# Attention over 32-token segments: one memory row per segment in place of eight, TensorE's order fixed by hand, and a reordered start

## Chip, cores, metric

One core of one Trainium2 chip. The metric is the device time of one execution in microseconds (us), the median of several runs.

## The reference, cut to what matters

```python
# x: (1, 2048, 1024); 32 heads of 128; segments of 32 tokens; 8 memory rows
xn = layernorm(x)
mem = mem0
for s in range(64):                      # one segment after the other
    h = concat([mem, xn[segment s]])     # 8 + 32 rows
    q, k, v = h @ Wq, h @ Wk, h @ Wv
    p = softmax(mask(q @ k.T) * scale)   # memory rows see all columns but later ones are masked
    o = (p @ v) @ Wo
    mem = o[:8];  out[segment s] = o[8:]
g = silu((sigmoid(xn @ w_gate) * (xn @ w_up)) @ w_down)
return x + out * g
```

The kernel does not walk the 64 segments in turn. It estimates each segment's memory from sums of V (in every segment but the first the eight memory rows come out equal), does all segments in parallel, checks at the end that the estimate was good, and has a sequential fallback for the case that it was not. The fallback is not taken with these inputs. The work is therefore almost all matmul: V, q and k projections, the attention itself, gate/up and down of the gated unit (GLU), and the output projection.

## The kernel before

Start: x goes out on the sync queue, Wv at the same time on the gpsimd queue; layernorm, transposition to xnT, then V.

```python
for t in range(NT):
    nc.sync.dma_start(xall[:, t, :], x2[t * P:(t + 1) * P, :])
...
for cg in range(8):
    nc.gpsimd.dma_start(wv_sb[:, :, cg * 512:(cg + 1) * 512], Wv2[...])
...
nc.sync.dma_start(xnT_dram, xnT[:])                 # 4 MB, read by the fallback alone
...                                                 # V, 4 token tiles at a time, two staging buffers
nc.sync.dma_start(vx_dram[t0 * P:(t0 + TG) * P, ...], v_sb[:])
```

Attention: three segments are packed into a tile of 3 x (32 tokens + 8 memory rows) = 120 rows; 22 tiles per head, in batches of at most 4. The text goes head by head, and a scheduler in the build decides the order of each engine's instructions.

```python
for h in heads:
    ...                                             # q and k projections of this head (psb tiles, ACT copies)
    for b0 in range(0, NT3, NB):                    # NB = 4
        for j in range(nb): nc.tensor.matmul(s_ps[:, j, :], lhsT=qt[...], rhs=kt[...])     # scores
        # softmax: DVE add mask, max, subtract; ACT exp; DVE sum, reciprocal, multiply -> pr_
        for j in range(nb): nc.tensor.transpose(pt_ps[:, j, :], pr_[:, j, :], ident[...])  # transposes
        nc.scalar.copy(pt[...], pt_ps[...])
        for j in range(nb): nc.tensor.matmul(o_ps[:, j, :], lhsT=va[...], rhs=pt[:, j, :]) # outputs
        ...                                         # ACT copy to otx, DVE copy of one memory row to omq
    ...                                             # now and then a unit of 64 GLU gate/up matmuls
```

After the last head come the remaining GLU units, the memory check (output projection of the memory rows, 256 matmuls), and the down and output projections.

## Time and profile before

| | before |
|---|---|
| median time | 1795.9 us (12 runs, 1794.1 to 1802.0) |
| span of the profiled run | 1793.8 us |
| TensorE busy | 96% |

The page's first part, of the kernel before: busy time, share of the span, number of instructions.

```profile
span 1793.8 us, 28090 instructions
...
PE 1724.6 (96%) x11673; PEld 884.1 (49%) x11673; DVE 831.8 (46%) x1989; ACT 569.6 (32%) x1243; POOL 22.1 (1%) x60
```

The 96% say little. A matmul's recorded duration is longer than the distance to the next one: the page gives 381 ns for one of 512 columns, while the next starts 216 ns later. Any wait of TensorE shorter than the difference does not show as idle time. The Trainium skill warns of exactly this ("Trainium Kernel Development and Optimization", § Performance Expectations: matmul busy time is a bad measure, because matmuls are pipelined), and this trace agrees. So I use another measure throughout: the distance from the start of one matmul to the start of the next. For each source line and column count I take the median distance and call the sum over all matmuls the *work*; what a stretch lasts beyond its work is its *waiting*.

The windows view of the kernel before, cut at the first and last matmul of each stage (start to the last V matmul; memory estimate; attention and the GLU after it; memory check to the end). Columns: stretch, length, busy time of each engine with instruction counts, granted clock, DMA share, GB/s.

```profile
0.00:277.90 277.90, 255.12 (x1659) 112.94 (x1660) 76.76 (x153) 57.15 (x96) 8.32 (x17) 0.99 0.40 142
277.90:427.10 149.20, 138.06 (x1295) 74.80 (x1294) 28.99 (x42) 23.40 (x39) 5.91 (x33) 0.99 0.59 183
427.10:1355.60 928.50, 903.44 (x6530) 497.44 (x6529) 654.35 (x1684) 469.95 (x1076) 7.39 (x8) 1.00 0.33 95
1355.60:1793.80 438.20, 427.99 (x2194) 198.91 (x2192) 71.70 (x110) 19.11 (x32) 0.49 (x2) 0.99 0.39 103
```

By the measure above these four stages hold 240.0, 133.9, 863.1 and 426.4 us of work. The waiting is 26.0 us in the first stage once the first matmul (at 12.2 us) has started, 14.9, 65.4 and 5.3 us.

### The profile page before, as it was taken

The page shows a single profiled execution, that of the slowest core. Times are in us where ns is not written, and L with a number is a line of the kernel's source. Part 1 is how long each engine was busy: PE and PEld are TensorE (multiplying, and loading weights), DVE is VectorE, ACT ScalarE, POOL GpSimd, SP SyncE. Part 2 cuts the span into 40 slices and gives each one's busy share as a digit, 9 for nine tenths or more (in the row PEclk, how much of TensorE's full clock was granted, in tenths as well). Part 3 has the DMA queues.
Part 4 walks back from the last instruction along what each step waited for, and adds up shares of the span by engine and source line. Part 5 has one row for each costly group of instructions (what it writes and reads, how often), then busy time and mean ns, then how long its engine had stood idle before and what let it go on. Part 6 is the DMA issues. An engine that isn't in the chain of part 4 may idle for free.

```text
span 1793.8 us, 28090 instructions
## 1 busy us (share of the span) xinstructions
PE 1724.6 (96%) x11673; PEld 884.1 (49%) x11673; DVE 831.8 (46%) x1989; ACT 569.6 (32%) x1243; POOL 22.1 (1%) x60
## 2 busy tenths in 40 slices
PE   5999998999999999999999999999999999999998
PEld 3344444544555555555555555555445444444443
DVE  7121211212967788767966778876512111111111
ACT  4111111112655455555655455555310000000000
POOL 1000000010000000000000000000100000000000
PEclk9999999999999999999999999999999999999999
DMA  9722216357223323313334332230464434443440
GB/s 335 251 71 71 71 71 223 107 191 163 77 83 89 89 76 98 104 40 85 77 89 133 80 77 70 68 88 36 184 262 112 124 98 103 108 124 89 98 122 25
DMA packets 220044, 200.06 MB, mean 112 GB/s; under 512 B 70528, under 2 KB 193408, under 8 KB 217736
## 3 DMA queue, kind: packets, MB, share of 16 engines
q1 hardware_dynamic: 213768, 174.10, 33.9%
q0 software_dynamic: 6144, 24.12, 3.6%
q8 instruction: 93, 1.52, 0.4%
q14 instruction: 39, 0.32, 0.1%
HBM read 133.19 MB, written 65.01 MB: 110 GB/s over the span
## 4 chain that ended last, share of the span: by engine, by line
PE 86%; DMA 6%; ACT 4%; DVE 3%; issue 1%; SPq 0%; ACTq 0%; DVEq 0%
PE pr L457 24%; PE a_ps L591 12%; PE v_ps L339 11%; PE y_ps L583 11%; PE u_ps L90 10%; PE g_ps L86 8%; PE o_ps L504 3%; PE pt_ps L499 2%; DMA wo_t<-in_A_Wo_dram 2%; ACT pt L501 2%; PE s_ps L480 2%; DMA xall<-in_A_x_dram 2%; PE sv_ps L346 1%; DMA vx_dram<-v_sb 1%; DVE ssum L491 1%
## 5 line engine op out<-in xcount | busy, mean ns | idle before, releaser
L457 PE MATMUL pr<-xnT,wq 128*128 128x480 bf16 (+1 forms) x1280 | 247.4, 336 | 0.0
L339 PE MATMUL v_ps<-wv_sb,xnT 128*128 128x512 bf16 x1024 | 242.2, 381 | 4.7 <-ACT v_sb L344 4.7
L457 PE MATMUL pr<-xnT,wk 128*128 128x480 bf16 (+1 forms) x1280 | 243.1, 336 | 0.0
L86 PE MATMUL g_ps<-xnT,wg 128*128 128x512 bf16 x896 | 228.3, 380 | 1.4 <-DVE vm_sb L393 1.2
L591 PE MATMUL a_ps<-wo_sb,ot 128*128 128x512 bf16 x1024 | 226.2, 379 | 0.0
L90 PE MATMUL u_ps<-xnT,wu 128*128 128x512 bf16 x896 | 222.2, 379 | 1.4 <-DVE hst L94 0.7
L583 PE MATMUL y_ps<-wd,ht 128*128 128x512 bf16 x896 | 200.5, 381 | 1.0 <-DMA ht<-hT_dram 1.0
L591 PEld LDWEIGHTS <-ot 128*128 128x128 bf16 x1024 | 100.2, 98 | 120.8
L457 PEld LDWEIGHTS <-wk 128*128 128x128 bf16 x1280 | 110.8, 98 | 86.2
L457 PEld LDWEIGHTS <-wq 128*128 128x128 bf16 x1280 | 111.3, 98 | 84.8
L586 ACT ACTIVATE th<-y_ps 128x512 f32<-128x512 f32 x32 | 19.1, 597 | 407.3 <-PE y_ps L583 407.3
L94 DVE SCALAR_TENSOR_TENSOR hst<-th,u_ps 128x512 bf16<-128x512 f32 x112 | 76.1, 681 | 155.9 <-PE u_ps L90 153.8
L583 PEld LDWEIGHTS <-ht 128*128 128x128 bf16 x896 | 87.8, 98 | 107.6 <-issue 1.6
L339 PEld LDWEIGHTS <-xnT 128*128 128x128 bf16 x1024 | 90.7, 97 | 93.3 <-issue 3.2
L501 ACT COPY pt<-pt_ps 120x480 bf16<-120x480 bf16 x192 | 101.2, 527 | 100.9 <-PE pt_ps L499 98.6
L90 PEld LDWEIGHTS <-wu 128*128 128x128 bf16 x896 | 84.2, 98 | 85.3 <-issue 1.9
L93 ACT ACTIVATE th<-g_ps 128x512 f32<-128x512 f32 x112 | 67.2, 600 | 182.2 <-PE g_ps L86 182.1
L342 DVE CAST v_sb<-v_ps 128x512 bf16<-128x512 f32 x64 | 44.0, 690 | 173.9 <-PE v_ps L339 163.4
L86 PEld LDWEIGHTS <-wg 128*128 128x128 bf16 x896 | 83.7, 98 | 80.9 <-issue 3.3
L460 ACT CAST qt<-pr 128x480 bf16<-128x480 f32 (+1 forms) x160 | 78.1, 498 | 128.9 <-PE pr L457 128.9
L489 ACT ACTIVATE e<-sm 120x480 f32<-120x480 f32 x192 | 107.7, 571 | 35.1 <-DVE sm L486 34.3
L482 DVE TENSOR_TENSOR sm<-s_ps,maskb 120x480 f32<-120x480 f32 x192 | 112.2, 609 | 10.4 <-PE s_ps L480 10.4
(679 smaller groups left out, 1580.2 us busy)
## 6 DMA issues: line engine op xcount, KB each, us to landing
wo_t<-in_A_Wo_dram SPq DMA_DIRECT2D x16, 1024.0 KB
vx_dram<-v_sb SPq DMA_DIRECT2D x32, 512.0 KB
oT_dram<-otx SPq DMA_DIRECT2D x16, 1024.0 KB
ot<-oT_dram SPq DMA_DIRECT2D x16, 1024.0 KB
va<-vx_dram SPq DMA_DIRECT2D x16, 1008.0 KB
hT_dram<-hst SPq DMA_DIRECT2D x28, 512.0 KB
ht<-hT_dram SPq DMA_DIRECT2D x16, 896.0 KB
wv_sb<-in_A_Wv_dram POOLq DMA_DIRECT2D x8, 1024.0 KB, 21.5
```

The costliest lines, as they stand in the source:

```text
L86: nc.tensor.matmul(g_ps[:], lhsT=wg[:, c, fc * P:(fc + 1) * P], rhs=xnT[:, c, tb * TB:(tb + 1) * TB], start=(c == 0), stop=(c == KC - 1))
L90: nc.tensor.matmul(u_ps[:], lhsT=wu[:, c, fc * P:(fc + 1) * P], rhs=xnT[:, c, tb * TB:(tb + 1) * TB], start=(c == 0), stop=(c == KC - 1))
L93: nc.scalar.activation(th[:], g_ps[:], ACTF.Tanh, scale=0.5)
L94: nc.vector.scalar_tensor_tensor(hst[:, :, fc, :], th[:].rearrange("p (a b) -> p a b", b=P), 1.0, u_ps[:].rearrange("p (a b) -> p a b", b= ...
L339: nc.tensor.matmul(v_ps[:], lhsT=xnT[:, c, t * P:(t + 1) * P], rhs=wv_sb[:, c, cg * 512:(cg + 1) * 512], start=(c == 0), stop=(c == KC - 1))
L457: nc.tensor.matmul(pr[:, 0:ntok], lhsT=w_[:, c, hh * DH:(hh + 1) * DH], rhs=xnT[:, c, tok0:tok0 + ntok], start=(c == 0), stop=(c == KC - 1))
L460: nc.scalar.copy(dst[:, bT:bT + bn, 0:TX], pr[:, 0:bn * TX].rearrange("p (T j) -> p T j", j=TX))
L482: nc.vector.tensor_tensor(sm[:, 0:nb, :], s_ps[:, 0:nb, :], maskb[:].unsqueeze(1).to_broadcast([TR, nb, TR]), op=ALU.add)
L489: nc.scalar.activation(e[:, 0:nb, :], sm[:, 0:nb, :], ACTF.Exp, scale=scale)
L501: nc.scalar.copy(pt[:, 0:nb, :], pt_ps[:, 0:nb, :])
L583: nc.tensor.matmul(y_ps[:], lhsT=ht[:, c, :], rhs=wd[:, c, hf * 512:(hf + 1) * 512], start=(c == 0), stop=(c == FC - 1))
L591: nc.tensor.matmul(a_ps[:], lhsT=ot[:, h, :], rhs=wo_sb[:, h, hf * 512:(hf + 1) * 512], start=(h == 0), stop=(h == H - 1))
```

## The change

A segment's eight equal memory columns act in the softmax like one column of eight times the weight, so one column with log 8 added to its scaled score can stand for them. `DEPTHS` holds, in us, D1 (from scores to transposes), D2 (from transposes to outputs) and GAP (before a head's first scores).

The intent: fewer rows in the attention matmuls, a TensorE order in which every softmax and copy has room, and a start in which x is not held up by Wv. GLU, V, down and output matmuls are the same.

```diff
-TM = SPT * M
-TR = TX + TM                       # 120 rows
+TR = TX + SPT                      # 99 rows
+LN8B = 2.0794415416798357 * (128.0 ** 0.5)
-NB = 4
+NB = 5
+DEPTHS = (4.5, 1.8, 0.6)
 # --- mask: a memory column stands for eight equal ones, so it gets + log 8
+    nc.gpsimd.memset(maskb[:, TX:TR], LN8B)
 # --- start
             nc.sync.dma_start(xall[:, t, :], x2[t * P:(t + 1) * P, :])
+            if extra_dma is not None and t == min(3, NT - 1):
+                extra_dma(0)       # first slice of Wv, same queue; the other seven after x
-        nc.sync.dma_start(xnT_dram, xnT[:])
+        nc.gpsimd.dma_start(xnT_dram, xnT[:])
-                    if t % 2 == 0:
+                    if t % 2 == 0 and cg > 0:
                         nc.vector.tensor_copy(v_sb[:, tl, :], v_ps[:])
-                nc.sync.dma_start(vx_dram[...], v_sb[:])
+                nc.gpsimd.dma_start(vx_dram[...], v_sb[:])
 # --- memory rows stored once, not eight times
-            nc.sync.dma_start(vm3[1:NSEG, ...], vm_sb[1:NSEG, 0, :].unsqueeze(1).to_broadcast([NSEG - 1, M, 512]))
+            nc.sync.dma_start(vm_dram[:, cg * 512:(cg + 1) * 512], vm_sb[0:NC, 0, :])
 # --- attention: projections and GLU become generators that yield after every matmul
+        def att_s(h, b): ...       # scores and softmax of batch b
+        def att_t(h, b): ...       # transposes and their copy
+        def att_o(h, b): ...       # outputs
+        with tc.manual_schedule(engines={mybir.EngineType.PE}):
+            ...
+            for h in range(H - 1):
+                for b in range(nbat):                        # 5 batches, spread over the head's period
+                    t0_ = now + GAP + b * (period - GAP) / nbat
+                    due += [(t0_, 0, h, b), (t0_ + D1, 1, h, b)]   # transposes D1 = 4.5 us later
+                for dt in region(h):                         # projections of head h + 1 and GLU chunks
+                    now += dt
+                    run_due()                                # outputs are due D2 = 1.8 us after transposes
 # --- segment 0, whose eight memory rows differ, is done apart for all heads at the end
+        for h0 in range(0, H, 8): ...
```

The clock `now` counts projection and GLU matmuls only.

## The prediction

> **What bounds it now.** The page shows TensorE busy 96% of 1793.8 us, but those ends are modelled, so I measured from one matmul's start to the next in the trace. Medians: 216 ns for 512 columns, 202 for 480, 56 for 128, 52 to 55 for 120, 32 for 72, 25 for 4. Time is streamed columns, as the Trainium skill says ("TensorE: Matmul & The Clock Gate": back to back, N columns cost about N cycles); the trace agrees. The medians sum to 1667 us. The rest: 12.2 us before the first matmul, about 7 after the last, 108 us of start-to-start time above the medians ("excess"): 17 before t = 70, 12 to 260, 15 from 260 to 400, 66 in attention (400 to 1290), 5 around the memory check (1350 to 1390). In attention it recurs per head pair: 0.9 us at a probability transpose, 0.8 at a gate matmul, 0.2 before many output matmuls, because each softmax follows its scores too closely in TensorE's in-order program.
>
> **What changes, costed.**
> 1. Eight equal memory rows per segment become one with a log 8 bias: tiles go from 120 to 99 rows, 22 to 21 per head; segment 0 is done apart (96 matmuls of 40 columns). 2112 score, transpose and output matmuls at 54 ns = 114 us become 2016 at an estimated 45 (between 32 for 72 columns and 54 for 120) plus 2.4 us. With the 96-column projection pieces TensorE's static sum falls 19 us, all critical.
> 2. TensorE's order in attention is fixed by hand: transposes 4.5 us after scores, outputs 1.8 us later, projection and GLU between. The softmax chain (four VectorE passes near 0.6 us, a 0.57 us Exp) takes under 4 us; VectorE falls to an estimated 64%. I expect 15 us of excess left of 66: gain 51, the largest term.
> 3. Start. Now x (sync queue) and Wv (gpsimd queue) share the DMA; the last x tile lands at 36.6 us at 360 GB/s. Afterwards x and the first Wv slice go first: x lands near 17 us, the first transpose is at 8.5 us instead of 12.2. LayerNorm (1.8 us a tile) and TensorE's 2.3 us a tile bound it then. Gain 15; but V stores now share the gpsimd queue, the third behind the 4 MB xnT store, which may stall V with its two buffers some 7 us near t = 55. Net 8.
> 4. Memory-row stores shrink from 4 MB to 0.6: gain 1. The rest is unchanged.
>
> Sum: 19 + 51 + 8 + 1 = 79 us.
>
> **Prediction: 1718 us, 8 in 10 between 1700 and 1740.** Faster by over 2%: 0.96; within 2%: 0.03; slower: 0.01.
>
> **What would show it.** Step 1: 2016 matmuls of 99 columns, 44 to 47 ns start to start. Step 2: waits of transposes on VectorE under 10 us; 23.9 us of matmul work per head, about 24.4 measured. Step 3: last x tile by 18 us; first V matmul by 12 us; V evictions waiting on a V store near 50 to 65 us. Step 4: no wait for weights at the memory check, as 52 us of GLU still cover them.
>
> **What would make it wrong.** Hand delays too short, so that every batch waits (32 heads x 5 batches x 0.3 us = 48 us); 99-column matmuls not scaling with columns; the V-store stall above 7 us; ScalarE's queue delaying the copies that free the four shared PSUM buffers.

## More of the kernel before

What waiting in attention looks like: the timeline of TensorE in the kernel before (start us, busy us, group of like instructions).

```profile
703.94 0.38 PE L86 MATMUL g_ps<-xnT,wg 128*128 128x512 bf16 x1
704.16 0.40 PE L499 MATMUL pt_ps<-ident,pr__7716 120*120 120x120 bf16 x4
704.39 0.81 PE L86 MATMUL g_ps<-xnT,wg 128*128 128x512 bf16 x3
705.20 0.37 PE L504 MATMUL o_ps<-pt,va 120*128 120x120 bf16 x4
705.41 0.38 PE L499 MATMUL pt_ps<-ident,pr__7749 120*120 120x120 bf16 x4
```

Between the four transposes at 704.16 and their outputs at 705.20 there are only three GLU matmuls. They need 3 x 216 = 648 ns, but from 704.39 to 705.20 it is 810 ns: TensorE stood for 160 ns until ScalarE had copied the transposes. The busy column covers it (0.81 us). That happens in most batches: matched batch by batch in the trace, the outputs begin within 0.1 us of the end of the copy in 162 of 192; the copy ends 0.87 us (median) after the start of the last transpose and the outputs begin 0.92 us after it. The waits view, which counts only visible idle time, has 11.2 us of it:

```profile
PE pt L65 <- DVE xn L62: 14.6, 3, 12.2
PE o_ps L504 <- ACT pt L501: 11.2, 18, 0.7
```

And the softmax itself is slow. VectorE's timeline in the kernel before:

```profile
760.05 0.17 DVE L493 RECIPROCAL rs<-ssum 120x4 f32<-120x4 f32 x1
760.14 0.62 DVE L485 TENSOR_REDUCE mx<-sm 120x4 f32<-120x480 f32 x1
760.68 0.65 DVE L495 TENSOR_TENSOR pr__8507<-e,rs 120x480 bf16<-120x480 f32 x1
...
761.48 0.65 DVE L486 TENSOR_TENSOR sm<-sm,mx 120x480 f32<-120x480 f32 x1
762.04 0.97 DVE L482 TENSOR_TENSOR sm<-s_ps,maskb 120x480 f32<-120x480 f32 x2
```

One pass takes about 0.65 us, but a reciprocal and a multiply of one batch (L493, L495) alternate here with the maximum and subtract of a second (L485, L486) and the mask of a third (L482): batches arrive in a bunch, and each is served between the others. From a batch's last score matmul to its finished probabilities it takes 9.4 us (median; 6.2 to 13.2).

## The result, and the profile after

| | before | after |
|---|---|---|
| median time | 1795.93 us (12 runs) | 1699.99 us (8 runs, 1696.2 to 1703.3) |
| ratio | | 0.9465, 95% interval 0.9454 to 0.9477 |
| span of the profiled run | 1793.8 us | 1698.1 us |

A ratio is the mean time of one kernel's fast runs over that of the other's of the same rounds, so not quite the ratio of the medians that are quoted.

The windows view of the changed kernel, cut at the same four stages:

```profile
0.00:264.30 264.30, 252.78 (x1660) 111.26 (x1660) 71.29 (x146) 61.66 (x104) 25.14 (x41) 1.00 0.42 150
264.30:411.40 147.10, 137.50 (x1294) 75.34 (x1293) 29.06 (x42) 23.64 (x39) 4.01 (x21) 0.99 0.58 175
411.40:1262.10 850.70, 850.18 (x6531) 474.04 (x6530) 591.43 (x1424) 434.84 (x896) 7.43 (x8) 1.00 0.33 96
1262.10:1698.10 436.00, 426.87 (x2194) 198.39 (x2192) 71.83 (x110) 19.11 (x32) 0.49 (x2) 0.99 0.36 104
```

By the starts of the matmuls at the cuts (the windows are rounded to 0.1 us) the first stage gained 13.7 us, the second 1.9, attention 77.9 and the last 2.1. In attention the work fell from 863.1 to 846.2 us (16.9) and the waiting from 65.4 to 4.4 us (61.0).

The waits view has nothing left of outputs on ScalarE, and 0.5 us of transposes on VectorE:

```profile
PE pt L70 <- DVE xn L67: 8.4, 1, 8.4
PE wos_ps L290 <- DMA wo_t<-in_A_Wo_dram: 7.4, 8, 1.3
PE sv_ps L386 <- DVE v_sb L382: 2.8, 1, 2.8
...
PE pt_ps L526 <- DVE pr__14533 L158: 0.5, 1, 0.5
```

TensorE's timeline in the changed kernel, one batch's outputs and the next batch's pieces:

```profile
706.21 0.35 PE L541 MATMUL o_ps<-pt,va 99*128 99x99 bf16 x4
706.40 0.57 PE L494 MATMUL pr<-xnT,wk 128*128 128x480 bf16 x2
706.81 1.89 PE L95 MATMUL g_ps<-xnT,wg 128*128 128x512 bf16 x8
708.53 0.35 PE L518 MATMUL s_ps<-kt,qt 128*99 128x99 bf16 x4
708.72 0.36 PE L494 MATMUL pr<-xnT,wk 128*128 128x480 bf16 x1
708.92 0.35 PE L526 MATMUL pt_ps<-ident,pr__8011 99*99 99x99 bf16 x4
709.11 1.92 PE L494 MATMUL pr<-xnT,wk 128*128 128x480 bf16 x15
710.87 0.23 PE L505 MATMUL pm<-cmT,wk 128*128 128x72 bf16 x2
710.93 0.35 PE L541 MATMUL o_ps<-pt,va 99*128 99x99 bf16 x4
```

The transposes of 708.92 have their outputs at 710.93, and ScalarE's copy between them ended at 709.86 (709.37 + 0.49): 1 us to spare. Every start follows its predecessor at the predecessor's own rate. VectorE now works on one batch at a time (the changed kernel; these are the scores of 708.53):

```profile
708.92 0.57 DVE L145 TENSOR_TENSOR sm<-s_ps,maskb 99x396 f32<-99x396 f32 x1 [0.90 <-PE s_ps L518]
709.53 0.57 DVE L147 TENSOR_REDUCE mx<-sm 99x4 f32<-99x396 f32 x1
710.13 0.57 DVE L148 TENSOR_TENSOR sm<-sm,mx 99x396 f32<-99x396 f32 x1
711.36 0.56 DVE L153 TENSOR_REDUCE ssum<-e 99x4 f32<-99x396 f32 x1 [0.66 <-ACT e L151]
...
712.17 0.57 DVE L158 TENSOR_TENSOR pr__8069<-e,rs 99x396 bf16<-99x396 f32 x1
```

Matched batch by batch over all batches (192 before, 160 after):

| median us | before | after |
|---|---|---|
| last score matmul to finished probabilities | 9.4 | 4.2 |
| last score matmul to first transpose | 10.2 | 5.0 |
| last transpose to end of its copy | 0.87 | 0.79 |
| last transpose to first output | 0.92 | 1.97 |

So the softmax, although it lasts less than half as long, also has its transposes waiting half as long after the scores. What grew is the room after the transposes, and the room that is left over: 0.9 us after the probabilities, 1.1 us after the copy.

### The profile page after: what moved, and what is told of

Its sections match the earlier page's. It is cut to its first block, busy times and chain, and to the rows that moved or that the text cites. A ratio compares the mean times of both kernels' runs of the same rounds, so it can differ in the third digit from the quotient of the medians.

```text
span 1698.1 us, 27515 instructions
## 1 busy us (share of the span) xinstructions
PE 1667.3 (98%) x11673; PEld 859.0 (51%) x11673; DVE 763.6 (45%) x1722; ACT 539.3 (32%) x1071; POOL 37.1 (2%) x72
## 4 chain that ended last, share of the span: by engine, by line
PE 95%; DMA 3%; DVE 1%; issue 0%; ACT 0%; DVEq 0%
PE pr L494 26%; PE a_ps L683 13%; PE v_ps L379 12%; PE y_ps L675 11%; PE u_ps L104 11%; PE g_ps L95 11%; DMA wo_t<-in_A_Wo_dram 2%; PE pt_ps L526 2%; PE s_ps L518 2%; PE o_ps L541 2%; PE sv_ps L386 1%; PE pm L505 1%; PE vmr_ps L428 1%; DMA vx_dram<-v_sb 1%; PE wos_ps L290 1%; PE wo_ps L274 0%
## 5 line engine op out<-in xcount | busy, mean ns | idle before, releaser
L494 PE MATMUL pr<-xnT,wk 128*128 128x480 bf16 (+2 forms) x1280 | 257.4, 336 | 0.0
L494 PE MATMUL pr<-xnT,wq 128*128 128x480 bf16 (+2 forms) x1280 | 257.0, 336 | 0.0
L95 PE MATMUL g_ps<-xnT,wg 128*128 128x512 bf16 x896 | 220.4, 379 | 0.0
L145 DVE TENSOR_TENSOR sm<-s_ps,maskb 99x396 f32<-99x396 f32 (+2 forms) x164 | 96.3, 587 | 66.7 <-PE s_ps L518 45.2
L153 DVE TENSOR_REDUCE ssum<-e 99x4 f32<-99x396 f32 (+2 forms) x164 | 95.6, 583 | 67.1 <-ACT e L151 66.5
L528 ACT COPY pt<-pt_ps 99x396 bf16<-99x396 bf16 (+1 forms) x160 | 81.0, 506 | 103.2 <-PE pt_ps L526 101.3
L151 ACT ACTIVATE e<-sm 99x396 f32<-99x396 f32 (+2 forms) x164 | 89.9, 548 | 67.2 <-DVE sm L148 65.1
L382 DVE CAST v_sb<-v_ps 128x512 bf16<-128x512 f32 x56 | 38.7, 692 | 158.4 <-PE v_ps L379 153.3
```

The source lines that it names most:

```text
L95: nc.tensor.matmul(g_ps[:], lhsT=wg[:, c, fc * P:(fc + 1) * P], rhs=xnT[:, c, tb * TB:(tb + 1) * TB], start=(c == 0), stop=(c == KC - 1))
L145: nc.vector.tensor_tensor(smv, s_ps, maskb.unsqueeze(1).to_broadcast([R, nb, W]), op=ALU.add)
L151: nc.scalar.activation(ev, smv, ACTF.Exp, scale=scale)
L153: nc.vector.tensor_reduce(ssum[0:R, 0:nb], ev, axis=AX.X, op=ALU.add)
L494: nc.tensor.matmul(pr[:, 0:ntok], lhsT=w_[:, c, hh * DH:(hh + 1) * DH], rhs=xnT[:, c, tok0:tok0 + ntok], start=(c == 0), stop=(c == KC - 1))
L528: nc.scalar.copy(pt[:, 0:nb, :], pt_ps[:, 0:nb, 0:TR])
```

## The experiments

All 15 runs were correct. The kernel before ran beside each group, at 1795.0 to 1795.6 us. The theory: in attention the spread order of TensorE removes the waiting, and the removed rows give their columns. The main rival: fewer elements and fewer batches relieved VectorE, and the order matters little.

### text_order: the changed kernel with attention written head by head

```diff
-        with tc.manual_schedule(engines={mybir.EngineType.PE}):
-            ...                       # the interleaving
+        for h in range(H):
+            for _ in proj(h): pass
+            for b in range(nbat):
+                att_s(h, b); att_t(h, b); att_o(h, b)
+            while glu_done < ((h + 1) * n_glu_h) // H: ...   # GLU chunks
```

> The changed kernel with its attention written head by head as before (projection, then every batch's scores, transposes and outputs, then GLU), no pinned order; tiles stay 99 rows, so the matmul work is that of the changed kernel. Theory A (the spread order made the gain in attention): the scores bunch again, the outputs come some 0.9 us after their transposes, and 40 to 60 us of waiting return: 1740 to 1760 us. Rival B (fewer and smaller softmax passes relieved VectorE, and the order matters little): under 1712 us.

Measured: 1749.7 us, 49.7 us above the changed kernel. The attention stage took 898.4 us with the same work (846.3 us), so 52.1 us of waiting are back:

```profile
413.00:1311.40 898.40, 893.60 (x6530) 463.73 (x6529) 533.72 (x1424) 424.09 (x896) 7.43 (x8) 1.00 0.31 92
```

The scores bunch again (the built order has the 21 score matmuls of a head's five batches within some 40 matmuls), the softmax lasts 8.4 us (median), and the outputs follow the last transpose after 0.87 us, as soon as the copy allows. The theory holds. 52.1 is less than the 65.4 us of before, but how much of the 13.3 us the rows took with them stays open: the built order is not that of before either (there the 22 score matmuls of a head lie within 76 matmuls), and the GLU comes in chunks of 8 matmuls in place of units of 64.

### sched_order: the interleaved text without the pin

```diff
-        with tc.manual_schedule(engines={mybir.EngineType.PE}):
+        with ExitStack():
```

> The changed kernel with its interleaved text but without the pin: the scheduler may reorder TensorE. Its order as built keeps scores about 5 us ahead of transposes and transposes about 1.8 us ahead of outputs. Theory A1 (how the text is interleaved is what counts): within 8 us of the changed kernel, 1700 to 1708 us. Theory A2 (the pin itself is needed): 1730 us or more.

Measured: 1701.4 us, attention stage 850.3 us. It is the interleaving of the text that counts; the scheduler, given that text, keeps nearly the same order.

### d1_short, d2_short, d1_long: the two distances

```diff
-DEPTHS = (4.5, 1.8, 0.6)
+DEPTHS = (3.5, 1.8, 0.6)      # d1_short
+DEPTHS = (4.5, 0.4, 0.6)      # d2_short
+DEPTHS = (6.0, 1.8, 0.6)      # d1_long
```

> The changed kernel with the distance from scores to transposes cut from 4.5 to 3.5 us. In the changed kernel's trace the softmax takes 4.19 us (median) from the last score matmul and has 4.97 us of room; with 1 us less room in each of 160 batches the missing time adds to 55 us. Theory A (TensorE waits exactly for what the chain lacks): 1740 to 1760 us, as waits of transposes on VectorE. Rival B: under 1712 us.

> The changed kernel with the distance from transposes to outputs cut from 1.8 to 0.4 us. The eviction of the transposes ends 0.79 us (median) after the last transpose and has 1.97 us of room; 1.4 us less leaves 0.3 us lacking in each of 160 batches, 47 us in sum. Theory A: 1735 to 1755 us, as waits of outputs on ScalarE. Rival B: under 1712 us.

> The changed kernel with the distance from scores to transposes raised from 4.5 to 6.0 us. Only 4.4 us of start-to-start time above the medians is left in attention. Theory A (no waiting is left to remove at 4.5): within 4 us of the changed kernel, 1696 to 1704 us. Rival: softmaxes of neighbouring batches now overlap on VectorE and lengthen each other, and waits return, 1715 us or more.

Measured: d1_short 1795.8 us, d2_short 1754.1 us, d1_long 1702.9 us.

With d1_short one microsecond less gives back the whole gain of the change: the attention stage took 945.5 us, 94.9 more. The direction and place are as expected (in all 160 batches the transposes start within 0.1 us of the finished probabilities), the size (55) is not. The reason is in the order: the clock counts projection and GLU matmuls only, and the microsecond that fell out of the window also held attention matmuls of other batches. In matmul work the room shrank from 4.96 to 3.74 us (medians), by 1.22, not 1.0. The softmax took 4.24 us, so about 4.24 + 0.06 - 3.74 = 0.56 us lack in each of 160 batches, 90 us.

With d2_short the attention stage took 904.7 us, 54.1 more (expected 47), and in all 160 batches the outputs start within 0.1 us of the end of the copy. The waits view of d2_short names it; the sum there is smaller because it sees only idle time:

```profile
PE o_ps L541 <- ACT pt L528: 30.1, 129, 0.3
```

With d1_long nothing is won: 849.8 us in attention. At 4.5 us hardly any wait was left.

### rows120, rows120_long, nb4: the rows

rows120 undoes the removal of rows inside the hand order (eight rows, no log 8, batches of 4, hence 6 per head); rows120_long gives it D1 = 6.0; nb4 keeps 99 rows and has 6 batches.

```diff
-TR = TX + SPT
+TM = SPT * M
+TR = TX + TM
-NB = 5
+NB = 4                        # nb4: this line alone
-DEPTHS = (4.5, 1.8, 0.6)
+DEPTHS = (6.0, 1.8, 0.6)      # rows120_long alone
 ...                           # mask, memory loads and copies as before, eight times
```

> The changed kernel with the eight equal memory rows per segment put back (tiles of 120 rows, no log 8 bias, memory rows stored and loaded eight times, batches of at most 4 tiles, so 6 per head), the order by hand kept. Theory A (the static step is columns, and the hand order has room for a longer chain): 2016 matmuls at 54 in place of 47 ns add 14 us, waits add 0 to 12: 1713 to 1727 us. Rival B (fewer softmax elements on VectorE are worth as much as the order): waits add 30 us or more, 1740 us and above.

> The 120-row tiles in the hand order (1744.4 us, 44 slower than the changed kernel where 14 were expected) with the distance from scores to transposes raised from 4.5 to 6.0 us. In its trace the softmax takes 4.70 us (median), up to 6.8, with 5.2 us of room. Theory C (the missing 30 us are softmaxes that outlast their room): waits mostly go, 1714 to 1726 us. Theory D (VectorE, busy 85% in that stage, cannot keep up with TensorE however far ahead the scores are): 1736 us or more.

> The changed kernel (99 rows) with at most 4 tiles in a batch, so 6 batches per head in place of 5, as the 120-row kernel has. Theory C/D (the rows' elements lengthen the softmax or load VectorE; the number of batches matters little): 1699 to 1707 us. Theory E (six batches, closer together, are what made the 120-row kernel wait): 1715 us or more.

Measured: rows120 1744.4 us, rows120_long 1724.1 us, nb4 1703.2 us. The first was a miss for the theory: 44 us, of which only 14 are columns. The windows view over the attention stage, rows120 first, then rows120_long:

```profile
413.60:1300.50 886.90, 867.33 (x6425) 491.89 (x6529) 704.77 (x1648) 462.48 (x992) 7.41 (x8) 1.00 0.36 97
```

```profile
414.60:1280.10 865.50, 865.35 (x6529) 494.46 (x6528) 704.97 (x1648) 452.39 (x992) 7.41 (x8) 1.00 0.36 99
```

VectorE's busy time is the same 705 us in both, so VectorE does keep up. With 120 rows the softmax takes 4.7 us (median), up to 6.8, and 5.2 us of room is not enough: 886.9 us less the work (860.4, from the trace of rows120_long, which has all its records) leaves 26.5 us of waiting. With 6.9 us of room 5.1 us are left. Six batches instead of five cost nothing by themselves (nb4: 849.5 us in attention). So the rows' second effect is on the length of the softmax, and a longer distance buys it off.

This gives a square of four attention stages (us), and below it a third row with the longer distance:

| | 120 rows | 99 rows |
|---|---|---|
| head by head | 928.5 (before) | 898.4 (text_order) |
| order by hand, D1 = 4.5 | 886.9 (rows120) | 850.6 (changed) |
| order by hand, D1 = 6.0 | 865.5 (rows120_long) | 849.8 (d1_long) |

At D1 = 4.5 the order is worth 41.6 us with 120 rows and 47.8 with 99; the rows are worth 30.1 us head by head and 36.3 in the order by hand. The third row changes the reading: with D1 = 6.0 the order is worth 63.0 us with 120 rows, and the rows only 15.7, little more than their 14.2 us of columns. What the rows gained beyond their columns in the order by hand was room for the softmax, and a longer distance gives the same. The upper row compares two head-by-head texts that were built into different orders (see text_order). The 99-row cells also have segment 0 apart and other batch sizes, and rows120 has 21 tiles plus segment 0 rather than 22, so the columns differ in a little more than rows.

### start_only and wv_pool: the start

start_only is the kernel before with the start's part of the diff. wv_pool is the changed kernel with Wv back on the gpsimd queue at once:

```diff
-            if extra_dma is not None and t == min(3, NT - 1):
+            if extra_dma is not None and t == 0:                                 # all eight slices issued here
 ...
-                nc.sync.dma_start(wv_sb[:, :, cg * 512:(cg + 1) * 512], ...)
+                nc.gpsimd.dma_start(wv_sb[:, :, cg * 512:(cg + 1) * 512], ...)   # all eight, beside x
```

> The kernel before with the new start alone (x and the first Wv slice first on one queue, V stores and the xnT store on the gpsimd queue, first V evictions all on ScalarE). In the two traces the last V matmul starts 13.6 us earlier afterwards. Theory A (the start's gain stands by itself and is handed on to the end): 10 to 16 us faster than before, 1779 to 1786 us. Rival (it is given back later, where the old attention order waits anyway): under 6 us, 1789 us or more.

> The changed kernel with Wv loaded as before, on the gpsimd queue beside x on the sync queue; all else of the new start kept. Theory A (the shared DMA delays x and is most of the start's gain): the last x tile lands near 36 us again, the last V matmul starts 8 to 14 us later, 1708 to 1715 us. Rival (moving the V stores and the first evictions is most of it): under 1704 us.

Measured: start_only 1785.0 us, 10.0 below the kernel before beside it; its last V matmul starts 12.5 us earlier, its last matmul 9.0 us earlier (the second stage and attention are 1.7 and 1.5 us longer than before). wv_pool 1714.4 us, 14.4 above the changed kernel and 12.6 above its second measurement (after_again); its last V matmul starts at 278.0 us (before: 277.9, after: 264.2). Moving this one load back undoes the whole gain of the start. Of the 13.8 us, 3.8 are lost before the first matmul (12.2 in place of 8.4 us) and 6.9 more up to the last transposes of xn, where the work waits for x; 2.4 more are lost after that, before t = 70, where a V store is again late (16.0 us to land). The lines of the x tile's view, in before, after and wv_pool; VectorE's first pass over x, with first and last start at the end:

```profile
L54 DVE BATCH_NORM_STATS2 st<-xall x32: 639/674/694, 3.8 to 40.2; 128x6 f32<-128x512 bf16 x32
...
  DMA xall<-in_A_x_dram: 10.8, 10
```

```profile
L59 DVE BATCH_NORM_STATS2 st<-xall x32: 636/672/695, 3.5 to 31.5; 128x6 f32<-128x512 bf16 x32
...
  DMA xall<-in_A_x_dram: 2.7, 2
```

```profile
L58 DVE BATCH_NORM_STATS2 st<-xall x32: 637/676/696, 3.5 to 39.5; 128x6 f32<-128x512 bf16 x32
...
  DMA xall<-in_A_x_dram: 9.9, 10
```

Two queues with work share the bandwidth. The Trainium skill says so ("DMA: Bandwidth & Descriptors", § Queues, rings and completion order: each DMA engine goes round between the queues that have work), and the runs agree: with Wv on a second queue VectorE waits for x ten times, with Wv behind x on the same queue twice.

### xnt_late, best, after_again, vbuf3, vbuf3_wo3: the V store that lands late

In the changed kernel V's matmuls lose 2.8 us at t = 53, while ScalarE and VectorE wait for a staging buffer whose V store took 12.8 us to land (median 3.4). xnt_late moves the text of the xnT store behind the V stage; best puts it on the sync queue and gives the streamed Wo three buffers; vbuf3 leaves the DMA alone and gives V three staging buffers; vbuf3_wo3 adds the third Wo buffer.

```diff
-        nc.gpsimd.dma_start(xnT_dram, xnT[:])
+        nc.sync.dma_start(xnT_dram, xnT[:])                                    # best
-        wos = es.enter_context(tc.tile_pool(name="vg_wo", bufs=2))
+        wos = es.enter_context(tc.tile_pool(name="vg_wo", bufs=3))             # best, vbuf3_wo3
-                v_sb = sb.tile([P, TG, 512], BF16, name="v_sb", tag="v_sb")
+                v_sb = sb.tile([P, TG, 512], BF16, name="v_sb", tag="v_sb", bufs=3)  # vbuf3, vbuf3_wo3
```

> The changed kernel with the 4 MB xnT store (needed by the fallback path alone) issued after the V stage, so that no V store queues behind it. In the changed kernel V's matmuls lose 2.8 us at t = 53 while the third V store takes 12.8 us to land instead of 3.4. Theory A (the xnT store ahead in the queue is the cause): that wait goes, 2 to 4 us faster than the changed kernel, 1694 to 1698 us. Rival (the loads of the other queue are the cause): the wait stays.

> The changed kernel with the xnT store on the sync queue, so that V stores no longer queue behind it on the gpsimd queue (the earlier edit for this did not move the store: the scheduler put it back third), and three buffers in place of two for the streamed Wo. Theory A (its place ahead in the same queue made the 2.8 us wait): no wait of V evictions on a V store; Wo waits of 7.4 us fall to 4 to 6: 1692 to 1697 us. Rival (the DMA's total load made it): the wait stays, 1697 us or more.

> The changed kernel itself, as the base on the same chip for the two runs beside it: 1697 to 1702 us, with the 2.8 us wait of V's matmuls near t = 53.

> The changed kernel with three V staging buffers in place of two; every DMA is issued as before. Theory F (the third V store is late because all loads and stores of that stretch share the DMA, and what turns lateness into a wait is having only two buffers): no wait of V evictions on a V store, 2 to 4 us faster than the changed kernel beside it. Rival (the wait has another cause, as moving the xnT store to the other queue already left it in place): the wait near t = 53 stays, within 1 us.

> As the run before, and three buffers in place of two for the streamed Wo. With three, the waits for Wo fell from 7.4 to 4.0 us and the stretch between V and the first projection from 147.2 to 143.3 us in the earlier run. If both savings stand side by side: 5 to 8 us faster than the changed kernel, 1691 to 1695 us. If one is handed back later: 2 to 4 us.

| | median us | ratio to before | interval |
|---|---|---|---|
| xnt_late | 1700.9 | 0.9472 | 0.9449 to 0.9495 |
| best | 1702.0 | 0.9477 | 0.9460 to 0.9494 |
| after_again | 1701.8 | 0.9480 | 0.9465 to 0.9494 |
| vbuf3 | 1694.8 | 0.9441 | 0.9423 to 0.9458 |
| vbuf3_wo3 | 1692.6 | 0.9428 | 0.9412 to 0.9444 |

xnt_late is inconclusive: the scheduler issued the store third in the queue as before, so nothing was moved. best moved it, and the wait did not go but grew; the waits view of best:

```profile
ACT v_sb L384 <- DMA vx_dram<-v_sb: 7.7, 1, 7.7
...
PE sv_ps L386 <- ACT v_sb L384: 6.7, 2, 6.3
...
PE wos_ps L290 <- DMA wo_t<-in_A_Wo_dram: 4.0, 4, 1.3
```

So its place behind the xnT store in the gpsimd queue is not needed to make a V store late: with the xnT store in the other queue one took 14.6 us to land. As the cause in the changed kernel it is not excluded: there the xnT store landed at 53.8 us and the late V store, next behind it in the queue, at 55.7. In each of these runs the 4 MB store was issued within 7 us of the late V store, and no run took it out of this stretch. The DMA was full in both, a share of 0.94 to 1.14 from t = 30 to 70 in the windows view, and at 0.2 from 100 to 200, where V stores land in 3.4 us. best's Wo waits did fall from 7.4 to 4.0 us; what it won there it lost at V. vbuf3 shows the rest: a V store still takes 12.4 us to land, but with a third buffer no eviction waits for it, the last V matmul starts at 260.9 us instead of 264.2, and the kernel is 7.0 us faster than after_again by the medians (in the traces the last matmul starts 3.0 us earlier; the execution of after_again that was profiled was the fastest of its six, 1699.5 us). With the third Wo buffer as well the last matmul starts 6.5 us earlier, at 1684.5: both savings stand. vbuf3_wo3 at 1692.6 us beats both kernels.

## Why the prediction was right or wrong

The mechanism and the order of the terms were right: faster by far more than 2%, most of it from attention's waiting, then columns, then the start. The size was off: 79 us forecast, 95.9 measured, and the measured median is just under the lower end of the range, 1700. A second measurement of the same kernel (after_again) gave 1701.8 us, so on which side of 1700 it falls says little; the sizes of the terms say more. Term by term, measured in the two traces:

| term | forecast | measured |
|---|---|---|
| columns of the attention matmuls | 19 | 16.9 |
| waiting in attention | 51 | 61.0 |
| start | 8 | 13.7 |
| memory-row stores | 1 | 1.9 (whole second stage; 146.3 to 150.2 us in other runs with one row and two Wo buffers, so not isolated) |
| end | 0 | 2.1 |
| sum | 79 | 95.6 (last matmul starts 95.6 us earlier) |

- **The step that failed: "I expect 15 us of excess left of 66".** 4.4 us were left, so the term was 61 and not 51. I had put 0.5 us of leftover waiting on each head without a trace to take it from. The softmax came out at 4.2 us and the room at 5.0 (d1_short and d1_long bracket it: 1 us less costs 95 us, 1.5 us more wins nothing), so all but a few batches fit: in 3 of 160 the transposes start within 0.1 us of the probabilities. The chain itself was longer than forecast: five full passes and a reciprocal, not "four VectorE passes", and 4.2 us, not "under 4". That it fitted is in part luck: the clock that sets D1 does not count attention matmuls, so the 4.5 us of the text became 5.0. The built order of the changed kernel could be read in advance, and matmul work between scores and transposes could have been summed from it (4.96 us) against five passes and an Exp of known length.
- **The second mis-sized term: the V-store stall, "some 7 us".** It was 2.8 us at the place named (V near t = 53), and it was not new: the kernel before lost 3.1 us of V's matmuls at t = 61, while VectorE and ScalarE waited 10.5 and 8.7 us for a V store. So it took next to nothing from the rest of the start's gain, which the prediction put at 15 and which came out near 13.7. The rest of the start was right: first transpose 8.4 us (8.5 forecast), first V matmul 11.4 us (by 12). wv_pool, which puts Wv beside x again and nothing else, loses 13.8 us in this stage, the whole gain. vbuf3 shows that having only two buffers turns the late store into a stall; that the loaded DMA makes it late is argued from its share, about 1 against 0.2. My reason for it, "the third behind the 4 MB xnT store" in one queue, is not needed for a stall (best), and neither shown nor excluded in the changed kernel.
- **The cause given for the old waiting, "each softmax follows its scores too closely", was wrong in its detail.** The transposes came 10.2 us after the scores; the softmax was stretched to 9.4 us because batches bunched on VectorE. More waiting stood before outputs than before transposes (34.6 against 16.8 us, summed from the distances before the first of each batch), because they followed the transposes after 0.92 us. d2_short shows what this costs, and text_order has both, the bunching and the early outputs. How the gain divides between the two distances when each alone is given to the kernel before was not tested.
- **At D1 = 4.5 the rows were worth more than their columns.** 99 columns cost 47 ns, at the upper end of 44 to 47. Head by head the rows gave 30 us and in the order by hand 36, of which 17 and 14 are columns. In the order by hand the rest is a softmax that fits its room (rows120, rows120_long). The forecast had put all of this waiting under the order; with D1 = 6.0, where the rows give 15.7 us, that split is right.
- **VectorE's load did not fall to 64%.** From t = 600 to 900 it was busy 221.7 of 300 us (74%), before 229.0 (76%): passes over 396 elements still take 0.57 us (480: 0.65), and the passes of a head now fit into less time. It did not matter, as rows120_long shows with 705 of 865.5 us.
- The end's 2.1 us are not explained by any edit there. From its first to its last matmul the stage took 431.4 us before and 429.3 after, and 428.3 to 435.2 us in the other runs, so it is within its spread. As forecast, the waits view shows no wait for weights at the memory check. Open are what makes the V store late, whether the second stage's 1.9 us are the memory-row stores, and how the order's gain divides between its two distances.

## What to carry to other kernels

When TensorE looks busy, measure from matmul start to matmul start: waits of 100 to 200 ns hide under modelled ends, and here those of 192 batches made most of 65 us. For each hand-over between engines write down two numbers, how long the other engine's chain takes and how much matmul work the order puts in between; below that length every missing tenth is paid once per batch, above it more distance is worth nothing. Before crediting a change's parts, run the square of them, and run it with more than one distance: at D1 = 4.5 the smaller work was worth over twice its columns, because it also shortened the chain; at 6.0 it was worth its columns and little more.

## What the Trainium skill lacked or had wrong

- "TensorE: Matmul & The Clock Gate", § Back-to-back issue gap, gives about 131 ns for N = 512 and 81 ns for N = 128 as the sustained spacing of weight-load and matmul pairs, and calls N/2.4 + 2.5 ns the isolated gap. Here every matmul has its own weight load, and the sustained medians are 216 ns (512), 202 (480), 56 (128), 47 (99), 42 (96), 32 (72) and 25 (4): the "isolated" formula and the 25 ns floor hold in the stream within 1 ns, except for 99 columns (43.8 by the formula); the 131 and 81 do not. Other sections of the same page do give 216 and 56 ns as the back-to-back spacing, so the page disagrees with itself.
- The same page, § What's actually happening, has TensorE start at half rate and change over after about 3.4 us of sustained activity, at a point that varies by 500 ns either way because the window of observation runs freely. The runs agree in the rate (427 ns for 512 columns). The point varied more: with the same start, gaps up to 0.35 us in it, the changed kernel was still at half rate 5.9 us after its first matmul, a transpose (8.44 to 14.36 us), and vbuf3 had left it after 3.7 us (8.75 to 12.41). The granted-clock column read 1.00 in that stretch of the changed kernel, so it does not show this start.
- "DMA: Bandwidth & Descriptors" tells how queues share the engines, but no page says how much later a store lands among loads. The same 512 KB V store landed in 3.4 us (median) where the DMA's share was 0.2, in 12.8 us where it was full with weight loads and a 4 MB store ahead of it in its queue, and in 14.6 us with the 4 MB store on the other queue.
